# The 18 stores of attention's output tiles: issued from ScalarE's queue instead of SyncE's

## The chip, the core and the metric

The kernel runs on one core of one Trainium2 chip. The time is that of one whole execution in device microseconds. The kernel before took 623.82 us, the median of three runs (621.92, 623.82 and 624.80).

## What is computed

Two layers follow each other. The first is an attention with two branches over q, k and v of shape 4 x 8 x 576 x 64: a "down" branch, in which means over groups of four positions attend to each other and the result is repeated four times, and a "local" branch, in which each position attends to those less than four positions away. The two are added. The second is a mixture of experts over the 2304 resulting rows of 512 numbers: noisy logits choose two of eight experts for each row, and each expert is a two-layer network, 512 to 1024 to 512.

```python
out_up = np.repeat(sm_attn(q_d, k_d, v_d), 4, axis=2)
scores = np.where(abs(pos[:, None] - pos[None, :]) < 4, q @ k.T * scale, -1e9)
x = rows_of(out_up + softmax(scores) @ v)                 # 2304 x 512
noisy = x @ w_gate + log1p(exp(x @ w_noise)) * noise
for e in range(8):                                        # top 2 of 8 for each row
    out[mask] += weight * (relu(x[mask] @ w1[e]) @ w2[e])
```

## The kernel before

**Attention, about the first 166 us.** The local branch goes in 20 blocks of 116 positions, five for each of the four batches. A block is a chain over four engines: scores on TensorE (l_qk), maximum and difference on VectorE (l_max), exponent on ScalarE (l_exp), sum (l_sum), normalisation, transpose (l_pt), copy by ScalarE (l_ptc), product with v (l_pv, L689), and the sum with the down branch on VectorE (l_x, L711). The v rows of block n are the tile vw; they come in four loads of 64 KB each that l_load_v issues from SyncE's queue (L629). l_pv takes all four in its first few products.

Rows are put together to 18 output tiles of 128 rows. Each is transposed on TensorE (l_xt, L720), copied by ScalarE into a buffer x (l_xtc, L726), and stored into the DRAM tile x_d, 256 KB (l_store, L730). Three buffers x stand in a ring. Below, x3 is the store of tile 3, vw7 the v rows of block 7. The router's steps follow each group of tiles (r_soft, L758 and L759, with its two table loads, to r_put, which scatters list entries), and the experts' gathers read x_d.

**Experts.** Weights are fetched in 256 KB pieces (fetch_w, L219 and L222, tile raw), split on ScalarE (L229) and VectorE (L234), and used by TensorE to the end of the program. Six fills of 768 KB (fill_out, L194) zero the output in the attention stage.

**Order.** A planner (run_steps, L302) works out the order of all steps from costs and priorities when the program is built. Each engine then runs its own list strictly in that order: an instruction that waits holds up all behind it on its engine. keep_warm (L399) puts filler products on TensorE where the planner expects a gap.

**DMAs from SyncE and ScalarE.** Each of them adds to one of eight semaphores, DMAHW0 to DMAHW7, which are handed out in turn. An issue waits until the DMA before it on its own semaphore has landed, so that at most eight are under way. This wait is made where the program is built, beside the waits for data and buffers.

The step's record names SyncE, and its planned place doesn't change with the engine that issues it:

```python
s_store += [Step("l_store", "sp", 0.45, lambda n=ck: l_store(n), after=[a11], use=[xb], move=1.0, **kw)]   # L1026
```

Of the kernel before, what the change touches and what calls it, by code (L numbers as in the profile page):

```python
# [22 lines left out]
def kernel(  # L23
# [12 lines left out]
    nc = tc.nc  # L36
# [3 lines left out]
    P = 128  # L40
# [56 lines left out]
    x_rows = x_d.rearrange("(t a) c -> t (a c)", a=4)  # L97
# [348 lines left out]
    st = {}  # L446
# [280 lines left out]
        st["x", n] = x  # L727

    def l_store(n):
        nc.sync.dma_start(out=x_rows[n * P : (n + 1) * P, :], in_=st.pop(("x", n)).rearrange("p a c i -> p (a c i)"))  # L730

    def l_lg(n):
        xT = st["xT", n]
# [191 lines left out]
    for b in range(B):  # L925
# [71 lines left out]
        for i in range(NB):  # L997
            n = NB * b + i
# [20 lines left out]
            for ck, g, c, w in ps_:  # L1019
                if g + w < P:  # L1020
                    continue
                ptxb, xb, lgb, lsb, plb = (buf(x_) for x_ in ("tp", "x", RG, "lgT", RS))
                kw = dict(light=True, prio=n + KX)
                a10 = Step("l_xt", "pe", 0.46, lambda n=ck: l_xt(n), cols=512, after=[s_x], use=[xTb[ck]], new=[ptxb], **kw)
                a11 = Step("l_xtc", "act", 0.49, lambda n=ck: l_xtc(n), after=[a10], use=[ptxb], new=[xb], **kw)
                s_store += [Step("l_store", "sp", 0.45, lambda n=ck: l_store(n), after=[a11], use=[xb], move=1.0, **kw)]  # L1026
                a12 = Step("l_lg", "pe", 0.35, lambda n=ck: l_lg(n), cols=2048, after=[s_x, s_sel] + s_wgn, use=[xTb[ck]], new=[lgb, lsb], **kw)
                a12 = Step("l_lgt", "act", 0.18, lambda n=ck: l_lgt(n), after=[a12], use=[lgb, lsb], **kw)
                a12 = Step("l_ls", "pe", 0.25, lambda n=ck: l_ls(n), cols=64, after=[a12], use=[lsb], new=[plb], **kw)
                st["lg_args", ck] = (a12, plb, n)  # L1030
# [594 lines left out]
```

## Time and profile before

| | us |
|---|---|
| median of three runs | 623.82 |
| lowest and highest | 621.92, 624.80 |
| the profiled execution's own time | 620.2 |
| its span in the profile | 618.5 |

The profile shows one execution. Its span is 1.7 us shorter than that execution's own time, and its time is 3.6 us under the median. TensorE is busy for 589.4 us of the span, VectorE 403.8, ScalarE 333.7, GpSimd 237.7. Issuing a DMA isn't counted as busy; it has rows of its own, under SPq for SyncE. The granted clock of TensorE has two levels in the rows, 1.00 (2.4 GHz) and 0.50 (1.2 GHz); values between are a mean over a stretch with both.

### The profile page before, as it was taken

How to read it: one execution, taken by the hardware profiler on the slowest of the kernel's cores; microseconds unless marked ns; L12 is line 12 of the kernel's file. 1: busy time of each engine (PE TensorE's matmuls, PEld its weight loads, DVE VectorE, ACT ScalarE, POOL GpSimd, SP SyncE). 2: the span in 40 equal slices, each digit the busy share in tenths (PEclk: the TensorE clock that was granted, in tenths of full speed). 3: DMA queues.
4: the chain of work that ended last, by engine and by line, in shares of the span. 5: the costliest groups of instructions: out<-in, count | busy, mean ns of one | idle time of the engine just before them, and what ended most of it. 6: DMA issues, size and time to landing. Idle time of an engine off the chain costs nothing. (4 is left out here: it accounts for less than half of the span.)

```text
span 618.5 us, 12836 instructions
## 1 busy us (share of the span) xinstructions
PE 589.4 (95%) x4579; PEld 508.2 (82%) x4579; DVE 403.8 (65%) x1054; ACT 333.7 (54%) x786; POOL 237.7 (38%) x318
## 2 busy tenths in 40 slices
PE   8899998998997899999999999999999999999995
PEld 7677776766886789987998898799789789878985
DVE  5999797897765534676487367647846865784421
ACT  7977876775542412674386167337726645752400
POOL 7585567762536233232423233232333223132111
PEclk9999998898798899999999999999999999999998
DMA  9997897987556562544454364444445445344301
GB/s 191 187 182 147 209 196 152 238 178 208 164 121 77 145 196 83 158 142 153 134 157 128 119 193 142 153 132 143 132 141 172 136 152 175 113 146 130 110 24 48
DMA packets 136101, 91.39 MB, mean 148 GB/s; under 512 B 72107, under 2 KB 118699, under 8 KB 136028
## 3 DMA queue, kind: packets, MB, share of 16 engines
q1 hardware_dynamic: 126076, 62.72, 42.4%
q0 software_dynamic: 9952, 27.77, 14.2%
q8 instruction: 37, 0.61, 0.4%
q14 instruction: 36, 0.29, 0.2%
HBM read 71.38 MB, written 19.38 MB: 147 GB/s over the span
## 5 line engine op out<-in xcount | busy, mean ns | idle before, releaser
L1407 PE MATMUL py<-w1h,h 128*128 128x512 f32 (+4 forms) x544 | 168.9, 388 | 0.6 <-DVE ga L1415 0.6
L1366 PE MATMUL ph<-xh,w0h 128*128 128x288 f32 (+3 forms) x448 | 133.8, 299 | 0.9 <-ACT low L1412 0.7
L1366 PE MATMUL ph<-xh,w0l 128*128 128x288 f32 (+3 forms) x448 | 133.7, 298 | 0.0
L1366 PE MATMUL ph<-xl,w0h 128*128 128x288 f32 (+3 forms) x448 | 133.6, 298 | 0.0
L1407 PEld LDWEIGHTS py<-w1h,h 128*128 128x128 f32 (+3 forms) x544 | 99.4, 186 | 26.3 <-ACT w1h L229 1.2
L1407 PE MATMUL py<-w1l,h 128*128 128x512 f32 (+5 forms) x288 | 111.4, 389 | 0.0
L1375 ACT ACTIVATE h<-ph 128x512 fp32r<-128x512 f32 (+3 forms) x88 | 42.6, 484 | 113.5 <-PE ph L1366 80.7
L1416 POOL DMA_INDIRECT out_dram<-ga,lt x35 | 38.2, 1093 | 153.8 <-DVE ga L1415 116.7
L1376 DVE SCALAR_TENSOR_TENSOR h<-ph,h 128x512 fp32r<-128x512 f32 (+3 forms) x88 | 48.0, 546 | 63.4 <-ACT h L1375 63.2
L1366 PEld LDWEIGHTS ph<-xh,w0h 128*128 128x128 f32 x448 | 84.4, 188 | 2.1 <-ACT low L1412 1.1
L1366 PEld LDWEIGHTS ph<-xl,w0h 128*128 128x128 f32 x448 | 84.4, 188 | 0.3
L1366 PEld LDWEIGHTS ph<-xh,w0l 128*128 128x128 f32 x448 | 84.3, 188 | 0.0
L1282 ACT ACTIVATE xr<-tr 32x128 f32<-32x128 f32 x220 | 67.8, 308 | 3.1
L229 ACT ACTIVATE w0h<-raw 128x512 fp32r<-128x512 f32 x64 | 39.2, 625 | 53.0 <-DMA raw<-in_moe_w_dram 52.9
L1383 POOL DMA_INDIRECT ga<-out_dram,cl x35 | 35.9, 1026 | 73.3 <-PE ph L1366 56.4
L1407 PEld LDWEIGHTS py<-w1l,h 128*128 128x128 f32 (+4 forms) x288 | 51.8, 180 | 14.0 <-DVE w1l L234 1.3
L1154 POOL DMA_INDIRECT gx<-x_d,cl x35 | 36.7, 1048 | 53.0 <-PE ph L1366 27.0
L234 DVE TENSOR_TENSOR w1l<-raw,w1h 128x512 fp32r<-128x512 f32 x64 | 44.0, 688 | 18.7 <-ACT w1h L229 18.4
L1415 DVE SCALAR_TENSOR_TENSOR ga<-py,lt,ga 128x512 f32<-128x512 f32 (+4 forms) x32 | 23.4, 733 | 50.1 <-PE py L1407 50.1
L897 POOL DMA_INDIRECT list_d<-pay,sli x36 | 36.8, 1022 | 48.7 <-PE ptl L674 12.2
L1284 DVE COPY xr<-tr 32x128 f32<-32x128 f32 x220 | 50.4, 229 | 2.7
L229 ACT ACTIVATE w1h<-raw 128x512 fp32r<-128x512 f32 x64 | 40.1, 627 | 18.5 <-DMA raw<-in_moe_w_dram 17.9
(208 smaller groups left out, 1007.6 us busy)
## 6 DMA issues: line engine op xcount, KB each, us to landing
raw<-in_moe_w_dram SPq DMA_DIRECT2D x128, 256.0 KB
vw<-in_v_dram SPq DMA_DIRECT2D x80, 64.0 KB
x_d<-x SPq DMA_DIRECT2D x18, 256.0 KB
out_dram<-zero SPq DMA_DIRECT2D x6, 768.0 KB
nat<-in_q_dram SPq DMA_DIRECT2D x16, 256.0 KB
nat<-in_k_dram SPq DMA_DIRECT2D x16, 256.0 KB
vg<-in_v_dram SPq DMA_DIRECT2D x8, 320.0 KB
vg<-in_v_dram SPq DMA_DIRECT2D x8, 256.0 KB
```

Source lines behind the costliest of these rows:

```text
L229: nc.scalar.activation(hi, raw, AF.Copy)
L234: nc.vector.tensor_tensor(lo, raws.pop((e, z, f)), hi.bitcast(F32), op=ALU.subtract)
L897: ins = nc.gpsimd.indirect_dma_start(out=list_d[:, :], out_offset=bass.IndirectOffsetOnAxis(ap=sli[:, kk, i : i + 1], axis=0), in_=pay[:, ...
L1154: ins = nc.gpsimd.indirect_dma_start(out=gx[: got(e, t)], out_offset=None, in_=x_rows[:, :], in_offset=bass.IndirectOffsetOnAxis(ap=lists[ ...
L1282: nc.scalar.activation(dst, src, AF.Copy)
L1284: nc.vector.tensor_copy(dst, src)
L1366: last_mm[0] = nc.tensor.matmul(ph[:, n, 0:nh], lhsT=w[:, c, :], rhs=xx[:, c, sl], start=(c == 0 and z == 0), stop=(c == NDC - 1 and z == 2))
L1375: nc.scalar.activation(hh, src, AF.Relu)
L1376: nc.vector.scalar_tensor_tensor(out=hl, in0=src, scalar=0.0, in1=hh.bitcast(F32), op0=ALU.max, op1=ALU.subtract)
L1383: after_pe(nc.gpsimd.indirect_dma_start(out=acc[: tok(e, t)], out_offset=None, in_=out[:, :], in_offset=bass.IndirectOffsetOnAxis(ap=cl[: ...
L1407: last_mm[0] = nc.tensor.matmul(py[:rows, js], lhsT=hx, rhs=w[:, js], start=(f == 0 and z == 0), stop=(f == NFC - 1 and z == len(terms) - 1))
L1416: nc.gpsimd.indirect_dma_start(out=out[:, :], out_offset=bass.IndirectOffsetOnAxis(ap=lt[:m, t, 0:1], axis=0), in_=acc[:m], in_offset=None ...
```

## The change

One line: l_store issues from ScalarE's queue.

```diff
     def l_store(n):
-        nc.sync.dma_start(out=x_rows[n * P : (n + 1) * P, :], in_=st.pop(("x", n)).rearrange("p a c i -> p (a c i)"))
+        nc.scalar.dma_start(out=x_rows[n * P : (n + 1) * P, :], in_=st.pop(("x", n)).rearrange("p a c i -> p (a c i)"))
```

The lists of TensorE, VectorE and GpSimd are the same. ScalarE's gains 18 rows, SyncE's loses 18. The semaphores are handed out anew. In each row stand the semaphores that it waits for; a DMA's own is among them.

First place, blocks 6 to 8. SyncE before: x_1357 is the tile of store x3, vw_1372 is vw7, vw_1424 is vw8.

```order
L629 DMA vw_1293<-in_v_dram 64x4x64 [waits DMAHW2_49]
L455 DMA nat_0_0_1_1331<-in_q_dram 128x8x64 [waits DMAHW3_49,PE_49]
L505 DMA vg_0_1_1355<-in_v_dram 64x4x256 [waits DMAHW4_49,Pool_49]
L629 DMA vw_1372<-in_v_dram 64x4x64 [waits DMAHW5_49]
L629 DMA vw_1372<-in_v_dram 64x4x64 [waits DMAHW6_49]
L629 DMA vw_1372<-in_v_dram 64x4x64 [waits DMAHW7_49]
L629 DMA vw_1372<-in_v_dram 64x4x64 [waits DMAHW0_49]
L730 DMA x_d<-x_1357 128x512 [waits DMAHW1_49,Activation_49]
L629 DMA vw_1424<-in_v_dram 64x4x64 [waits DMAHW2_49,PE_49]
```

In the order of before the store x3 stands behind the four loads of vw7. SyncE now, from the last load before vw6 on:

```order
L455 DMA nat_0_0_0_1279<-in_q_dram 128x8x64 [waits DMAHW6_49,PE_49]
L629 DMA vw_1293<-in_v_dram 64x4x64 [waits DMAHW0_49]
L629 DMA vw_1293<-in_v_dram 64x4x64 [waits DMAHW1_49]
L629 DMA vw_1293<-in_v_dram 64x4x64 [waits DMAHW2_49]
L629 DMA vw_1293<-in_v_dram 64x4x64 [waits DMAHW3_49]
L455 DMA nat_0_0_1_1331<-in_q_dram 128x8x64 [waits DMAHW4_49,PE_49]
L505 DMA vg_0_1_1355<-in_v_dram 64x4x256 [waits DMAHW6_49,Pool_49]
L629 DMA vw_1372<-in_v_dram 64x4x64 [waits DMAHW7_49]
L629 DMA vw_1372<-in_v_dram 64x4x64 [waits DMAHW0_49]
L629 DMA vw_1372<-in_v_dram 64x4x64 [waits DMAHW1_49]
```

SyncE's turn skips 7 and 5: those are stores. ScalarE now, at the same place:

```order
L612 ACTIVATE up_1353<-od_1_1378 128x288 [waits PE_49]
L612 ACTIVATE up_1353<-od_2_1383 128x288 [waits PE_49]
L612 ACTIVATE up_1353<-od_3_1388 128x288 [waits PE_49]
L730 DMA x_d<-x_1357 128x512 [waits DMAHW7_49,Activation_49]
L792 ACTIVATE wts_1400<-wts_1400 128x8 [waits DVE_49]
```

The store x3 has semaphore 7, and the next DMA on 7 is the first load of vw7.

Second place, blocks 17 to 19. SyncE before: x_2777, x_2830 and x_2873 are the tiles of stores x12, x13 and x14, vw_2763 is vw18, vw_2847 is vw19.

```order
L629 DMA vw_2763<-in_v_dram 64x4x64 [waits DMAHW2_49,PE_49]
L629 DMA vw_2763<-in_v_dram 64x4x64 [waits DMAHW3_49]
L629 DMA vw_2763<-in_v_dram 64x4x64 [waits DMAHW4_49]
L629 DMA vw_2763<-in_v_dram 64x4x64 [waits DMAHW5_49]
L730 DMA x_d<-x_2777 128x512 [waits DMAHW6_49,Activation_49]
L629 DMA vw_2847<-in_v_dram 64x4x64 [waits DMAHW7_49,PE_49]
L629 DMA vw_2847<-in_v_dram 64x4x64 [waits DMAHW0_49]
L629 DMA vw_2847<-in_v_dram 64x4x64 [waits DMAHW1_49]
L629 DMA vw_2847<-in_v_dram 64x4x64 [waits DMAHW2_49]
L730 DMA x_d<-x_2830 128x512 [waits DMAHW3_49,Activation_49]
L730 DMA x_d<-x_2873 128x512 [waits DMAHW4_49,Activation_49]
```

Here x12 stands behind all of vw18, and x13 and x14 behind all of vw19. SyncE now, from the second of the last three fills on (vw_2673 is vw17):

```order
L194 DMA out_dram<-zero 1536x1x128 [waits DMAHW4_49]
L194 DMA out_dram<-zero 1536x1x128 [waits DMAHW6_49]
L629 DMA vw_2673<-in_v_dram 64x4x64 [waits DMAHW7_49,PE_49]
L629 DMA vw_2673<-in_v_dram 64x4x64 [waits DMAHW1_49]
L629 DMA vw_2673<-in_v_dram 64x4x64 [waits DMAHW3_49]
L629 DMA vw_2673<-in_v_dram 64x4x64 [waits DMAHW4_49]
L629 DMA vw_2763<-in_v_dram 64x4x64 [waits DMAHW5_49,PE_49]
L629 DMA vw_2763<-in_v_dram 64x4x64 [waits DMAHW6_49]
L629 DMA vw_2763<-in_v_dram 64x4x64 [waits DMAHW7_49]
L629 DMA vw_2763<-in_v_dram 64x4x64 [waits DMAHW0_49]
L629 DMA vw_2847<-in_v_dram 64x4x64 [waits DMAHW2_49,DMAHW1_49,PE_49]
L629 DMA vw_2847<-in_v_dram 64x4x64 [waits DMAHW2_49]
```

SyncE's turn now skips 5, 0 and 2. ScalarE now:

```order
L742 ACTIVATE lgT_2819<-pl_2814 128x128 [waits PE_49,Activation_49]
L730 DMA x_d<-x_2777 128x512 [waits DMAHW5_49,Activation_49]
L726 ACTIVATE x_2830<-ptx_2820 128x4x4x32 [waits DMAHW7_49,PE_49]
L726 ACTIVATE x_2873<-ptx_2860 128x4x4x32 [waits DMAHW3_49,PE_49]
L742 ACTIVATE lgT_2881<-pl_2876 128x128 [waits PE_49,Activation_49]
L758 ACTIVATE sp_2894<-lg_2852 128x16 [waits DVE_49]
L759 ACT_TABLE_LOAD
L759 ACTIVATE sp_2894<-sp_2894 128x16 [waits Activation_49]
L730 DMA x_d<-x_2830 128x512 [waits DMAHW0_49]
L730 DMA x_d<-x_2873 128x512 [waits DMAHW2_49]
L679 ACTIVATE pT_2887<-ptl_2882 128x512 [waits PE_49]
```

The stores x12, x13 and x14 have 5, 0 and 2. The next DMAs on these are the first and the fourth load of vw18 and the second of vw19, on SyncE.

## Rows read from the trace of the kernel before

**Rows 1.** The page: span, and busy time of each engine.

```profile
span 618.5 us, 12836 instructions
PE 589.4 (95%) x4579; PEld 508.2 (82%) x4579; DVE 403.8 (65%) x1054; ACT 333.7 (54%) x786; POOL 237.7 (38%) x318
```

**Rows 2.** Stretches: length, busy PE, PEld, DVE, ACT, POOL; clock, DMA share, GB/s.

```profile
55.00:166.00 111.00, 101.78 (x1432) 80.58 (x1429) 88.99 (x312) 78.16 (x186) 64.19 (x96) 0.91 0.82 192
166.00:210.00 44.00, 36.75 (x232) 33.07 (x230) 26.11 (x92) 17.22 (x35) 18.58 (x30) 0.95 0.56 103
210.00:618.50 408.50, 400.87 (x2317) 355.01 (x2316) 243.05 (x552) 195.02 (x460) 116.20 (x110) 0.99 0.44 136
```

**Rows 3.** Shorter stretches of attention, the same columns.

```profile
70.00:76.00 6.00, 6.00 (x74) 4.79 (x73) 4.78 (x22) 4.78 (x11) 2.54 (x4) 1.00 0.76 190
...
82.00:94.00 12.00, 11.81 (x161) 9.01 (x161) 11.18 (x35) 8.85 (x34) 8.05 (x12) 1.00 1.02 186
...
103.00:113.30 10.30, 7.47 (x47) 6.35 (x45) 6.34 (x24) 6.76 (x15) 5.38 (x9) 0.50 0.86 173
...
144.00:152.00 8.00, 7.44 (x154) 6.34 (x150) 7.03 (x35) 4.77 (x10) 2.11 (x3) 1.00 0.62 157
```

**Rows 4.** The store's line: count, ns least, median and most, first and last start.

```profile
L730 SPq DMA_DIRECT2D x_d<-x x18: 319/547/1327, 58.3 to 166.1; - x18
```

**Rows 5.** SyncE's issues in order of time: start and length in us, line, count.

```profile
70.89 3.23 SPq L629 DMA_DIRECT2D vw<-in_v_dram  x4
74.22 0.55 SPq L730 DMA_DIRECT2D x_d<-x  x1
...
83.71 0.80 SPq L730 DMA_DIRECT2D x_d<-x  x1
...
85.75 2.59 SPq L629 DMA_DIRECT2D vw<-in_v_dram  x4
...
90.62 2.15 SPq L629 DMA_DIRECT2D vw<-in_v_dram  x2
...
93.58 0.56 SPq L730 DMA_DIRECT2D x_d<-x  x1
...
98.23 1.33 SPq L730 DMA_DIRECT2D x_d<-x  x1
...
100.31 0.61 SPq L219 DMA_DIRECT2D raw<-in_moe_w_dram  x1
...
136.69 5.45 SPq L194 DMA_DIRECT2D out_dram<-zero  x3
...
145.98 1.28 SPq L629 DMA_DIRECT2D vw<-in_v_dram  x2
...
149.32 1.20 SPq L629 DMA_DIRECT2D vw<-in_v_dram  x1
```

**Rows 6.** SyncE's waits between 89 and 92 us: total, times, longest.

```profile
SPq L629 <- DMA x_d<-x: 0.8, 1, 0.8
```

**Rows 7.** ScalarE in order of time; in brackets idle time before, and its releaser.

```profile
71.69 0.99 ACT L612 ACTIVATE up<-od 128x288 f32<-128x288 f32 x3
...
105.63 0.63 ACT L229 ACTIVATE w0h<-raw 128x512 fp32r<-128x512 f32 x1 [4.89 <-DMA raw<-in_moe_w_dram]
...
135.05 0.23 ACT L759 ACTIVATE sp<-sp 128x32 f32<-128x32 f32 x1
...
151.02 0.22 ACT L759 ACTIVATE sp<-sp 128x16 f32<-128x16 f32 x1
```

**Rows 8.** TensorE in order of time, the products with v (l_pv).

```profile
78.16 1.14 PE L689 MATMUL o<-pT,vw 64*64 64x58 f32 x32
...
96.25 1.21 PE L689 MATMUL o<-pT,vw 64*64 64x58 f32 x28 [0.16 <-DMA vw<-in_v_dram]
...
149.44 1.14 PE L689 MATMUL o<-pT,vw 64*64 64x58 f32 x32
...
154.74 1.74 PE L689 MATMUL o<-pT,vw 64*64 64x58 f32 x26 [2.53 <-DMA vw<-in_v_dram]
```

## The prediction

> **What bounds the kernel now.** I read the busy line of the page first, then a table of stretches, then SyncE's, ScalarE's and TensorE's instructions in order of time around a few stores, and the waits of SyncE last. TensorE is busy for 95% of the span [rows 1]. Attention, 55 to 166 us, has TensorE busy for 101.8 of 111 us, and what follows for 36.8 of 44 and 400.9 of 408.5 [rows 2]. TensorE's list is fixed, and nearly all of it after 166 us hangs on attention, so what attention loses the whole kernel loses. ScalarE, which gets the stores, idles 33 of the 111 us (78.2 busy); VectorE idles 22. SyncE is the hidden one: it issues back to back for long stretches and each of its issues also waits for its semaphore. I therefore look less at what 18 issues cost than at which load now waits for which store.
>
> **What the change removes and adds.** SyncE loses 18 issues, median 0.547 us [rows 4]: 9.8 us. ScalarE gains 18 such issues. How long one takes there no row shows; I take SyncE's 0.55, bounds 0.32 and 1.33 [rows 4]. Each waits in its queue for two things: the copy l_xtc, which stands some instructions ahead on the same engine, and a load that was issued eight DMAs earlier and has landed when ScalarE gets there. So the stores hardly wait. They leave no later than before where SyncE was behind with them. Only loads, the list of SyncE, and behind them TensorE, can be late.
>
> The eight semaphores make them late. Before, a store took its place in SyncE's queue behind the loads of the same turn. Now the store takes an earlier place in the turn, and the load that comes eight later waits for it to land, while the store itself waits for ScalarE to arrive. At both places that the order shows, a load of v waits for a store which ScalarE reaches after SyncE would have issued that load.
>
> How long from the end of an issue to the landing? Least: vw17's last load ends its issue at 145.98 + 1.28 = 147.26 and is used at 149.44 without a wait, so 2.2 us at most [rows 5, 8]. vw18's last: 150.52 to 154.74, 4.2 us, waited for [rows 5, 8]. The raw weights: 100.92 to 105.63, 4.7 us [rows 5, 7]. Most: a store issued at 83.71 + 0.80 = 84.51, for which SyncE waited until 90.62, 6.1 us [rows 5, 6]. I use 2.2 to 6.1 as bounds. The short one belongs to a stretch with a DMA share of 0.62, the long one to a share of 1.02 [rows 3].
>
> *vw7.* The store x3 stands behind the three copies that end at 71.69 + 0.99 = 72.68 [rows 7]; issued by 73.2; the share there is 0.76 [rows 3], nearer to 0.62, so 2.5 us: landed at 75.7. vw7's first load started at 70.89 [rows 5]; now at 75.7, 4.8 us later. Four issues take 4 x 0.64 = 2.6 (two take 1.28 at 145.98, rows 5), to 78.3, and 2.2 more to land: 80.5. l_pv of block 7 started at 78.16 [rows 8], and TensorE is busy without a gap there (6.00 of 6.00, rows 3). **+2.3 us**; bounds 1.8 (issue of 0.32 and 2.2) and 9.8 (6.1 twice).
>
> *vw9.* SyncE goes on late. It catches up by three slots of stores that are gone, 0.55 for x3 [rows 5], the median 0.55 for x4 [rows 4], 0.80 for x5 [rows 5]: 1.9 of 4.8, so 2.9 late when vw9 is due (85.75, rows 5). vw9 had nothing to spare: TensorE waited for it at 96.25 [rows 8]. TensorE is itself 2.3 late by then. Net 0.6 at least; but the DMA engines are full there (1.02, rows 3), and a load that waits for another late load adds to it, up to 2.6. **+1.0**, bounds 0 and 2.6.
>
> *Raw weights: something is given back.* ScalarE idles 4.89 us at 105.63 for weights issued at 100.31 [rows 5, 7]. SyncE is rid of x6 and x7 before them, 0.56 + 1.33, so of its 2.9 about 1.0 is left there, while ScalarE is 3.3 late. The wait shrinks by the difference. **-2.0**, bounds 0 and -4.9.
>
> *vw17.* The first of three fills now waits for x11, which stands behind the table work that ends at 135.28 [rows 7]: with 1.3 of lateness so far, 0.55 and 2.5, 139.6 in place of 136.69 [rows 5]. That is 2.9 late, 1.6 more than TensorE, and vw17 stands behind the fills with nothing to spare at 149.44. The fills' issue is long (5.45 for three, rows 5), held up by full DMA engines, and takes up part. **+0.8**, bounds 0 and 2.9.
>
> *vw18, the largest.* Its last load waits for x13 to land. x13 stands behind the table work that ends at 151.02 + 0.22 = 151.24 [rows 7]; issued by 151.8, landed 2.2 later at 154.0, the load issued by 154.6, landed 4.2 later (what this very load took): 158.8. Before, TensorE got it at 154.74 after a wait of 2.53 [rows 8]. **+4.1**; bounds 2.1 (2.2 twice) and 9.9 (6.1 twice). Lateness from earlier places moves ScalarE and TensorE alike and doesn't enter.
>
> *ScalarE's own time.* 9.8 us of issues against 33 us of idle time; where it waits for TensorE or VectorE an issue costs nothing, and in the few dense runs the copies behind it come half a microsecond later. **+0.3**, bounds 0 and 9.8 (no issue hidden).
>
> The Trainium skill, "DMA: Bandwidth & Descriptors", section "Issuing engines are not separate DMA queues", says that issuing from a second engine only saves the sequencer's issue time, since all queues run on the same DMA engines. By that alone the change would be worth at most the slots above and never a loss; the order rows show what the rule leaves out, that a shared turn of semaphores ties the two queues together.
>
> **The sum.** 2.3 + 1.0 - 2.0 + 0.8 + 4.1 + 0.3 = 6.5 us. The profiled execution took 620.2, so 626.7 by its own measure; the median of the runs shown is 3.6 above it, 623.8, so I forecast **630.3 us**, with 625 to 636 as this case's own range (all low bounds but the give-back at its full size would even give -1.0; the high ends cannot all meet, since each late stretch empties the DMA engines for the next).
>
> **Rivals.**
> 1. *The lateness is taken up.* SyncE's late loads find emptier DMA engines and land in 2.2 us where they took 4.7 to 6.1. For it: a share of 1.02 just before vw9. Against it: vw18 sits in a stretch where even quick landings give +2.1. Only that and a little of vw7 is left beside the -2.0: +0.7, 624.5 us.
> 2. *Faster.* SyncE's freed slots bring the raw weights in early enough that ScalarE's idle 4.89 us goes and with it the stretch from 103.0 to 113.3 in which the granted clock is 0.50 (1.2 GHz) after TensorE had run out of work [rows 3, 7]. At full clock its 7.47 us of work are 3.7, and its 2.8 us of gap go: -6.5, 617.3 us. It decides if the raw load starts 4 us or more before 100.31 against ScalarE's list. For it: three stores, 2.7 us of issue (0.80, 0.56 and 1.33, rows 5), stood ahead of it from 83.71 on. Against it: the 4.8 us lost at vw7. The Trainium skill, "Perfetto Trace Analysis", section "DMA Optimizations", speaks for this one: it advises one issuing engine for inputs and another for outputs. No row of before bears it out for loads that share a turn with stores.
> 3. *Slower by the clock.* The new gaps at 78, 96 and 156 us are as long as those after which the clock fell in rows 3. Each such stretch costs 3.7 us (7.47 halved). Two of them on top of the forecast are 7.4 more, 637.7 us. Against it: a single gap may be under 2.5 us.
>
> **How the numbers follow.** Forecast 0.50, first rival 0.20, faster 0.13, clock 0.17. A measurement of this kernel tells about 0.5%, 3.1 us, from no change: faster is under 620.7, slower over 626.9. Faster: 0.13 of the second rival and 0.01 of the first, 0.14. Same: 0.16 of the first and 0.04 of the forecast, 0.20. Slower: the rest, 0.66. The range leaves out half of the faster case and some of the clock's: 619 to 638.
>
> **What would show it.** vw7's first load starts near 75.7 instead of 70.89, and rows of SyncE waiting for x_d<-x are there by the dozen. TensorE waits for vw at blocks 7, 9 and 18, the last for 6 us instead of 2.53. ScalarE's wait for raw falls from 4.89 to about 3. The first experts' products come 6 to 7 us later than at 166 us, and from there on the two traces run alike. If vw18's wait stays at 2.5 us, the largest term is wrong; if the low clock after 103 us is gone, the second rival has it.

## The result: 1.2% slower, as forecast

Eight runs of the changed kernel had a median of 630.28 us (626.51 to 631.88), eight of the kernel before 622.65 us (617.81 to 625.60). The ratio is 1.0124, with a 95% interval of 1.0082 to 1.0166, so +7.7 us (5.1 to 10.3). A second comparison later, of four runs with seven, gave 1.0161 (1.0102 to 1.0220). The profiled execution after took 631.72 us, the one before 620.2. They differ by 11.5 us, more than the medians do; a single profile is one draw from a range of several us, and the section on why comes back to this.

Page of the kernel after, its span and busy times. It answers to [rows 1].

```profile
span 629.8 us, 12832 instructions
PE 592.1 (94%) x4579; PEld 510.3 (81%) x4579; DVE 402.4 (64%) x1054; ACT 333.2 (53%) x786; POOL 236.9 (38%) x318
```

Stretches of the kernel after, with the limits of [rows 2] moved to where the same work stands now. Columns: length, busy PE, PEld, DVE, ACT, POOL; clock, DMA share, GB/s.

```profile
55.00:177.50 122.50, 105.75 (x1435) 82.96 (x1435) 87.28 (x312) 77.59 (x185) 63.80 (x96) 0.87 0.75 174
177.50:221.50 44.00, 36.07 (x233) 32.75 (x232) 25.21 (x92) 16.78 (x33) 18.13 (x30) 0.96 0.54 97
221.50:629.80 408.30, 400.28 (x2321) 354.34 (x2319) 244.22 (x554) 196.43 (x464) 115.94 (x110) 1.00 0.44 137
```

In this profile attention takes 122.5 us where it took 111, and what follows takes what it took: all is lost before 177.5 us. The DMA share fell from 0.82 to 0.75: the same 21.3 MB (192 GB/s x 111 us, 174 x 122.5) are moved over a longer time.

The store's line after, from its own view: count, ns least, median and most, first and last start. It answers to [rows 4].

```profile
L730 ACTq DMA_DIRECT2D x_d<-x x18: 326/326/589, 55.1 to 178.8; - x18
```

SyncE's issues after, in order of time (start, length, line, count), for [rows 5].

```profile
75.68 5.27 SPq L629 DMA_DIRECT2D vw<-in_v_dram  x8
...
89.30 15.12 SPq L629 DMA_DIRECT2D vw<-in_v_dram  x12
...
105.16 0.60 SPq L219 DMA_DIRECT2D raw<-in_moe_w_dram  x1
...
144.30 4.95 SPq L194 DMA_DIRECT2D out_dram<-zero  x3
149.35 17.34 SPq L629 DMA_DIRECT2D vw<-in_v_dram  x12
```

SyncE's waits of the kernel after between 50 and 180 us: total, times, longest.

```profile
SPq L629 <- DMA x_d<-x: 15.1, 7, 3.9
...
SPq L455 <- DMA x_d<-x: 3.9, 2, 3.6
```

The same view of the kernel before:

```profile
SPq L629 <- DMA x_d<-x: 1.2, 2, 0.8
```

SyncE now waits 19.0 us for stores, where it waited 1.2; in a second profile of the kernel before (e8 below) it is 0.7. vw7's first load starts at 75.68 instead of 70.89. The twelve loads of vw9 to vw11 take 15.12 us of SyncE; with a store between them they took 12.4 us in the first profile of before and 14.3 in e8, so little of that is new.

ScalarE of the kernel after, in order of time; the ACTq rows are the stores x3 and then x13 and x14.

```profile
71.66 0.39 ACT L612 ACTIVATE up<-od 128x288 f32<-128x288 f32 x1
71.71 0.33 ACTq L730 DMA_DIRECT2D x_d<-x  x1
71.95 0.70 ACT L612 ACTIVATE up<-od 128x288 f32<-128x288 f32 x2
...
112.44 0.63 ACT L229 ACTIVATE w0h<-raw 128x512 fp32r<-128x512 f32 x1 [5.50 <-DMA raw<-in_moe_w_dram]
...
158.38 1.28 ACT L759 ACT_TABLE_LOAD   x1
158.41 0.95 ACTq L730 DMA_DIRECT2D x_d<-x  x2
```

x3 is issued at 71.71 and SyncE's load starts at 75.68, when it has landed: 3.6 us from the end of the issue. ScalarE's wait for raw weights is 5.50 us where it was 4.89 [rows 7].

TensorE of the kernel after, the products with v that waited, for [rows 8].

```profile
80.23 1.02 PE L689 MATMUL o<-pT,vw 64*64 64x58 f32 x26 [0.43 <-DMA vw<-in_v_dram]
...
99.46 2.10 PE L689 MATMUL o<-pT,vw 64*64 64x58 f32 x30 [1.81 <-DMA vw<-in_v_dram]
...
165.06 0.47 PE L689 MATMUL o<-pT,vw 64*64 64x58 f32 x2 [4.26 <-DMA vw<-in_v_dram]
166.02 0.46 PE L689 MATMUL o<-pT,vw 64*64 64x58 f32 x2 [0.49 <-DMA vw<-in_v_dram]
167.66 1.75 PE L689 MATMUL o<-pT,vw 64*64 64x58 f32 x26 [1.18 <-DMA vw<-in_v_dram]
```

Block 18 now waits 4.26 + 0.49 + 1.18 = 5.9 us for v, in place of 2.53.

### The profile page after: what moved, and what is told of

Its sections match the earlier page's. It is cut to its first block, busy times and chain, and to the rows that moved or that the text cites. A ratio compares the mean times of both kernels' runs of the same rounds, so it can differ in the third digit from the quotient of the medians.

```text
span 629.8 us, 12832 instructions
## 1 busy us (share of the span) xinstructions
PE 592.1 (94%) x4579; PEld 510.3 (81%) x4579; DVE 402.4 (64%) x1054; ACT 333.2 (53%) x786; POOL 236.9 (38%) x318
## 3 DMA queue, kind: packets, MB, share of 16 engines
q0 software_dynamic: 9952, 27.77, 14.3%
```

## The experiments

The theory is that of the prediction: loads on SyncE wait for stores on ScalarE through the shared turn of eight semaphores. Rival A is ScalarE's time for 18 issues. Rival B is the stores' data, which leave on a queue of their own and meet the loads in the DMA engines. All ratios are to runs of the kernel before on the same chip.

### Six stores of each kind (e1, e2)

```diff
-        nc.sync.dma_start(out=x_rows[...], in_=...)
+        (nc.scalar if n in (1, 2, 9, 15, 16, 17) else nc.sync).dma_start(out=x_rows[...], in_=...)   # e1
+        (nc.scalar if n in (3, 4, 8, 12, 13, 14) else nc.sync).dma_start(out=x_rows[...], in_=...)   # e2
```

> Six stores (x1, x2, x9, x15, x16, x17) are issued from ScalarE, the other twelve from SyncE. By the trace of before each of the six is issued, with 2.2 us to land, before SyncE reaches the load that has the semaphore next (at most 0.1 us late). Theory (shared turn: loads wait for late stores): no loss, ratio to before 0.995 to 1.003, the products of block 7 and 18 start as in before (78.2 and 151.8, wait for v near 2.5 us at block 18). Rival A (ScalarE pays for issuing): a third of the loss of the full change, 2.5 us, ratio 1.004. Rival B (stores leave earlier and collide with loads): the same third.

> Six stores (x3, x4, x8, x12, x13, x14) are issued from ScalarE, the other twelve from SyncE. By the trace of before the loads that have the semaphores next are vw7 (4.5 us late), vw8 (3.2), vw13 (0.3), vw17 (3.2) and two of vw18 (5.3 and 4.6). Theory (shared turn): nearly the whole loss with a third of the stores: +2 us at block 7 and +5 to +8 at blocks 17 and 18, ratio 1.008 to 1.016. Rivals A (ScalarE's issue time) and B (earlier stores collide): like the six others, +2.5 us, ratio 1.004.

Measured: e1 1.0051 (1.0019 to 1.0084), e2 1.0070 (1.0045 to 1.0095). The pair doesn't tell the theories apart: e1 lost more than the theory said, e2 a little less, and the 1.004 of the rivals lies just under e2's interval. The six of e1 were not free. SyncE in e1, waits and issues between 60 and 75 us:

```profile
SPq L458 <- DMA x_d<-x: 4.6, 1, 4.6
```

```profile
63.34 0.60 SPq L458 DMA_DIRECT2D nat<-in_q_dram  x1
68.60 0.60 SPq L458 DMA_DIRECT2D nat<-in_k_dram  x1
```

The load after 63.34 shares with x2 and waited 4.6 us: x2 took 6.0 us from the end of its issue to landing, where 2.2 had been reckoned.

### ScalarE's time alone (e3)

```diff
         nc.sync.dma_start(out=x_rows[...], in_=...)
+        for _ in range(2):
+            nc.scalar.activation(junk, ident[:, 0:2], AF.Copy)
```

> All 18 stores stay on SyncE; at each store's place ScalarE gets two small ACTIVATEs on two columns instead, about 0.2 us each, 0.4 us a store against the 0.33 that an issue on ScalarE took. Rival A (ScalarE's time is what the change costs): +7 us, ratio 1.010 to 1.014. Theory (shared turn): 0 to +2 us, ratio 1.000 to 1.003.

Measured: 1.0016 (0.9982 to 1.0051), against 1.0124 for the change. The row shows that ScalarE had more to do than with the stores, 36 x 0.203 = 7.3 us against 18 x 0.326 = 5.9:

```profile
L733 ACT ACTIVATE junk<-ident x36: 187/203/226, 54.8 to 171.1; 128x2 f32<-128x2 f32 x36
```

Rival A falls as the main cause; at most 0.5% is left to it.

### The stores from GpSimd (e4), and the turn without the stores (e9)

GpSimd's DMAs have eight other semaphores of their own in these traces. e4 takes the stores out of the turn; e9 puts 18 DMAs of two numbers each, issued from ScalarE at the stores' places, back in. In e9's trace 226 of the first 228 DMAs of SyncE have the semaphore that they have in the change.

```diff
-        nc.sync.dma_start(out=x_rows[...], in_=...)
+        nc.scalar.dma_start(out=tie_d[n : n + 1, :], in_=st["x", n][0:1, 0, 0, 0:2])   # e9 alone
+        nc.gpsimd.dma_start(out=x_rows[...], in_=...)                                  # e4 and e9
```

> All 18 stores are issued from GpSimd, which has semaphores of its own for DMAs; SyncE's loads then share their turn with no store. Theory: no load of SyncE waits for a store; block 7 starts as in before or earlier, block 18 waits at most 2.5 us for v; what GpSimd pays for 18 issues (about 1 us each by its indirect ones) may come back elsewhere, ratio 0.99 to 1.01. Rival B (stores that leave earlier collide with loads in the DMA engines): the waits for v as in the changed kernel, 9 us over eight places, ratio 1.01 or more.

> The 18 stores go from GpSimd as in e4_pool (0.996 of before), but at each store's place ScalarE issues a DMA of two numbers from the same tile x into a scratch row. These take the places in the turn of the eight semaphores that the stores have in the changed kernel, load by load, and move no data to speak of. Theory (shared turn): the loss comes back without the stores, ratio to before 1.006 to 1.016; SyncE waits 8 to 19 us for the small DMAs, TensorE again for v. Rival B (a store on ScalarE's queue costs by its data, which shares the DMA engines with the loads): as e4_pool, ratio 0.993 to 1.000.

Measured: e4 0.9961 (0.9932 to 0.9989), e9 1.0074 (1.0042 to 1.0107). In e4 no load of SyncE waits for a store, TensorE has no wait for v among those listed after 50 us, and ScalarE's wait for raw weights is nearly gone. ScalarE's waits in e4 between 50 and 180 us, of that kind:

```profile
ACT w0h L229 <- DMA raw<-in_moe_w_dram: 1.2, 2, 1.1
```

In e9 SyncE waits again, 8.5 us for 36 numbers in all. SyncE's waits in e9, 50 to 180 us:

```profile
SPq L630 <- DMA tie_d<-x: 7.3, 5, 3.7
...
SPq L456 <- DMA tie_d<-x: 1.2, 1, 1.2
```

SyncE's issues in e9, with a hole of 3.7 us in front of vw7 where the change has one of 4.0, and then ScalarE's issue that SyncE waited for:

```profile
69.86 0.60 SPq L506 DMA_DIRECT2D vg<-in_v_dram  x1
74.16 5.30 SPq L630 DMA_DIRECT2D vw<-in_v_dram  x8
```

```profile
71.97 0.20 ACTq L731 DMA_DIRECT2D tie_d<-x  x1
```

Of the hole, 1.5 us went by until ScalarE issued the small DMA and 2.2 until it had landed. The stores' data and their place are those of e4, so 1.0074 / 0.9961 = 1.011 (about 1.007 to 1.016 by the two intervals), some 7 us, come with the small DMAs. They carry no data to speak of (rival B), and e3 says that ScalarE's time for them isn't it (rival A). What is left is the turn. This rests on the medians: the profiles are of the slowest of e4's twelve runs (625.24, median 619.18) and of the fastest of e9's (622.74, median 627.09), so they show who waits for whom, not what it costs. From e9 to the change there is another 1.0124 / 1.0074 = 1.005, which the two intervals don't set apart from 1: a whole store lands later than two numbers, and its data may cost something too; no run parts these.

### A few instructions later (e5)

```diff
     def l_ptc(n):
         nc.scalar.activation(st["pT", n], st.pop(("ptl", n)), AF.Copy)
+        put_stores()          # nc.scalar.dma_start of the tiles copied since
```

> All 18 stores are issued from ScalarE as in the changed kernel, but x0 to x14 a few instructions later in its list: behind the next copy l_ptc, and the last three at once. In the new turn no load is given the semaphore of a store that ScalarE reaches late, except the last load of vw7 (1.9 us late by the times of before, against 4.5 for its first) and one of vw19 (0.5). Theory (shared turn): most of the loss goes, ratio to before 0.994 to 1.004; SyncE waits for stores under 5 us in all, and block 18's wait for v is at most 3 us. Rival A (ScalarE's 18 issues): as slow as the changed kernel, ratio 1.010 to 1.015. Rival B (stores and loads collide): 1.006 to 1.015.

Measured: 1.0135 (1.0081 to 1.0189). The expectation failed: nothing was gained. SyncE waited 14.6 us for stores, not under 5. The largest of its waits, from a window of 104 to 112 us, and ScalarE at that time:

```profile
SPq L455 <- DMA x_d<-x: 6.5, 1, 6.5
```

```profile
104.08 0.60 ACT L477 ACTIVATE qT<-pt 128x512 f32<-128x512 f32 x1 [4.83 <-PE pt L466]
104.09 0.83 ACTq L740 DMA_DIRECT2D x_d<-x  x2
```

x6 and x7 stood behind a copy that waited 4.83 us for TensorE. A store put off in ScalarE's list takes over the waits of that list, and SyncE takes over the store's. The run doesn't separate the theories, since its premise, a turn without late stores, didn't come about.

### The early twelve and the late six (e6, e7)

As in e1, with n < 12 in e6 and n >= 12 in e7.

> Only x0 to x11 are issued from ScalarE; their turn up to the fills is that of the changed kernel, and no load of vw17 to vw19 shares with a store of ScalarE. Theory: the lateness before block 17 as in the changed kernel (+2 at block 7, +5 to +7 at block 11, +7 to +9 at block 16), without the +4 at block 18; ratio 1.006 to 1.011. Rival A: two thirds of the loss, 1.008, but spread evenly, 0.4 us a store.

> Only x12 to x17 are issued from ScalarE. Now x12 shares with the last load of vw17 (3.2 us late), x13 and x14 with the last two of vw18 (5.3 and 4.6). Theory: nothing moves before block 17, then +3 at block 17 and +2 to +4 at block 18: ratio 1.006 to 1.010 from six stores. Rival A: a third, 1.004.

Measured: e6 1.0138 (1.0089 to 1.0187), e7 1.0045 (1.0009 to 1.0082). Both are slower. By the medians most of the loss belongs to the first twelve, more than the theory had said, and the last six cost less than it had said; but both intervals overlap the theory's ranges, and they are too wide to add the two up.

### Both kernels once more (e8, e12)

> The kernel before once more, for a second profile of it: which of its waits repeat. Both theories: the start of block 7 within 0.5 us, the wait for vw18's last load between 1 and 4 us, ScalarE's wait for raw weights between 3 and 6 us; the time within 0.6% of 622.

> The changed kernel once more, for a second profile of it. What the shared turn causes must repeat: SyncE waits 10 to 20 us in all for stores, the products of block 7 end 1.3 to 2.3 us later than in both profiles of before, SyncE holds vw18's last load until x13 has landed, and from the end of block 16 to the end of block 18 at least 1 us more is lost than in the second profile of before (2.6 us). What is chance need not: the waits for v at blocks 9 and 10. Ratio to before 1.008 to 1.017.

Measured: e8 took 625.46 us; its wait at block 18 was 0.83 + 0.57 = 1.4 us, in reach of the 1 to 4 expected, and ScalarE's for raw weights 5.3. e12 has the ratio 1.0161 given above. Its block 7 lost 0.9 us and missed the 1.3 to 2.3; from the end of block 16 to that of block 18 it lost 5.2. SyncE's waits in e12 and then in e8, 50 to 180 us:

```profile
SPq L629 <- DMA x_d<-x: 15.6, 7, 5.2
...
SPq L455 <- DMA x_d<-x: 1.2, 1, 1.2
...
SPq L194 <- DMA x_d<-x: 0.4, 1, 0.4
```

```profile
SPq L629 <- DMA x_d<-x: 0.7, 1, 0.7
```

TensorE's waits for v in e12 and then in e8, same stretch:

```profile
PE o L689 <- DMA vw<-in_v_dram: 10.9, 8, 4.0
```

```profile
PE o L689 <- DMA vw<-in_v_dram: 3.9, 3, 2.5
```

So the change makes it 9.0 and 10.9 us where the two profiles of before have 2.7 and 3.9. These waits alone don't prove a loss, though: e3, in which no store is moved and whose profiled execution took 621.25 us, has

```profile
PE o L690 <- DMA vw<-in_v_dram: 7.0, 6, 2.6
```

What goes along with the loss is SyncE's wait for stores (50 to 180 us, in us; in e9 for the small DMAs). With one profile a run this is an order, not a law:

| run | SyncE's wait | TensorE's wait for v | ratio to before |
|---|---|---|---|
| before, e8 | 1.2, 0.7 | 2.7, 3.9 | 1 |
| e3, e4 (all stores on SyncE; all on GpSimd) | 0.6, none | 7.0, none | 1.0016, 0.9961 |
| e7 | 2.1 | 6.4 | 1.0045 |
| e1 | 6.8 | 6.2 | 1.0051 |
| e9 | 8.5 | 4.4 | 1.0074 |
| e6 | 8.8 | 9.1 | 1.0138 |
| e2 | 10.5 | 8.3 | 1.0070 |
| e5 | 14.6 | 5.9 | 1.0135 |
| the change, e12 | 19.0, 17.2 | 9.0, 10.9 | 1.0124, 1.0161 |

### Two attempts at a better kernel (e10, e11)

Both start from e4, the stores on GpSimd.

```diff
-        nc.sync.dma_start(out=rows, in_=zero...)                 # e10, fill_out
+        nc.gpsimd.dma_start(out=rows, in_=zero...)
-        Step("fill_out", ..., after=[s_fills], ...)              # e11
+        Step("fill_out", ..., after=[s_fills] + ([s_x] if f >= 3 else []), ...)
```

> The 18 stores and the six fills of 768 KB are issued from GpSimd, so SyncE holds loads alone. If the loads of v are late because SyncE is held up behind fills and stores: faster than with the stores alone, ratio to before 0.988 to 0.996. If the fills then crowd the DMA engines in front of the loads in the same way, or GpSimd pays for their descriptors: 0.995 to 1.005.

> The 18 stores are issued from GpSimd, and the last three fills are planned behind the last block of the local branch, so that vw17 to vw19 go ahead of them; the planner works the other steps out anew. If the fills are what makes vw17 and vw18 late: ratio 0.985 to 0.995. If the new order or the raw weights behind the fills cost as much: 0.995 to 1.01.

Measured: e10 0.9965 (0.9936 to 0.9995), e11 1.0015 (0.9986 to 1.0043). The fills gain nothing on top of e4, either way; in e11 the planner also built another order, so it says nothing of the fills alone. e4, all stores on GpSimd, is the fastest version of the study, by 0.4%, a little under what a run of few repeats can tell.

## Why the prediction was right, and where its terms were not

The forecast was +6.5 us, the ratio says +7.7 and, in the second comparison, about +10. Sign and mechanism were right, the places only in part. That the time forecast, 630.3 us, and the median measured, 630.28, agree so closely is luck: the kernel before came out at 622.65 in these runs, not at 623.82, and the change cost over 1 us more. The terms are checked on two profiles of each kernel (620.2 and 625.46 us before, 631.72 and 633.69 after), by how much later than in the first profile each block's last product with v ends. A row is the growth of that lateness over a stretch; the last column is the mean of the two after less the mean of the two before.

| stretch | e8 | after | e12 | predicted | measured |
|---|---|---|---|---|---|
| up to the end of block 6 | 0.2 | -0.1 | -0.1 | 0 | -0.2 |
| block 7 (vw7) | 0.0 | 2.0 | 0.9 | 2.3 | 1.5 |
| blocks 8 to 10 (vw9) | 4.9 | 4.0 | 6.8 | 1.0 | 2.9 |
| blocks 11 to 13 (raw weights) | 0.6 | 0.7 | 1.2 | -2.0 | 0.7 |
| blocks 14 to 16 | -2.0 | 2.2 | -2.8 | 0 | 0.7 |
| blocks 17 and 18 (vw17, vw18) | 2.6 | 4.0 | 5.2 | 4.9 | 3.3 |
| from there to the experts | -0.4 | -0.9 | 2.4 | 0.3 | 0.9 |
| sum | 5.9 | 12.0 | 13.5 | 6.5 | 9.8 |

With two profiles a side a row is good to two or three microseconds, since e8 alone, the same kernel, stands 5.9 us behind the first.

Two experiments lend a third profile of each side up to block 16: until then SyncE's loads have the semaphores of before in e7 and those of the change in e6. Their rows are 0.0 and 0.9 for block 7, 3.3 and 6.7 for blocks 8 to 10, -0.6 and -0.9 for blocks 11 to 13, -2.3 and 0.1 for blocks 14 to 16. So block 7 alone is clear of chance: 0.0 in each profile without the change, 0.9 to 2.0 with it. In blocks 8 to 10 the first profile of before, on which the forecast was built, was a good draw; the two others lose 4.9 and 3.3 us there without any change.

- *vw7* came as forecast: its first load started at 75.68, where 75.7 was forecast. That was luck, for two errors met there. The store was taken to leave at 73.2, behind three copies; it left at 71.71, while those copies were still to run, and then took 3.6 us to land, not 2.5. The row is 1.5, where 2.3 was forecast.
- *vw17 and vw18* were 4.9 together and came to 3.3; the place held in the first profile only. There x13 left by 158.74; SyncE's next load on its semaphore is vw18's last. Two narrow windows of SyncE in the kernel after:

```profile
157.93 2.14 SPq L629 DMA_DIRECT2D vw<-in_v_dram  x3
```

```profile
161.96 4.73 SPq L629 DMA_DIRECT2D vw<-in_v_dram  x5
```

  The second begins with that last load, 3.2 us after x13's issue ended, and TensorE's wait is 5.9 us, where 6 was forecast. In e12 the last load waited for x13 too, but TensorE's long wait stands at block 17, 4.03 + 1.34 us, and at block 18 it is 0.60:

```profile
159.45 0.63 PE L689 MATMUL o<-pT,vw 64*64 64x58 f32 x4 [4.03 <-DMA vw<-in_v_dram]
161.42 2.07 PE L689 MATMUL o<-pT,vw 64*64 64x58 f32 x28 [1.34 <-DMA vw<-in_v_dram]
...
165.59 2.00 PE L689 MATMUL o<-pT,vw 64*64 64x58 f32 x28 [0.60 <-DMA vw<-in_v_dram]
```

- *The raw weights* are the step that failed. I had SyncE 1.0 us late there, ScalarE 3.3, and 2.0 given back (the difference is 2.3; the sum has a slip of 0.3). The row is +0.7: nothing came back. Against the first profile SyncE was 4.85 late, 105.16 against 100.31 [rows 5], and ScalarE waited 5.50 us. But most of this isn't the change's doing. In e8, the kernel before, the same load leaves at

```profile
104.11 0.60 SPq L219 DMA_DIRECT2D raw<-in_moe_w_dram  x1
```

  In e12 it leaves at 105.95, and ScalarE waited 2.9 (e8: 5.3). On the means of two profiles, block 10 ends 4.2 us later than before and this load leaves 3.3 later, so SyncE gains under 1 us on the rest where 2.3 had been reckoned; ScalarE's wait falls from 5.1 to 4.2, and none of that reaches TensorE. Why it doesn't stays open.
- *vw9* was too small, 1.0 where the row is 2.9. What was mis-sized is the time to landing in the stretch with full DMA engines [rows 3]. x6 left by 90.06 + 0.33, and vw10's second load, which has its semaphore now, starts at 99.09:

```profile
99.09 3.94 SPq L629 DMA_DIRECT2D vw<-in_v_dram  x6
```

  That is 8.7 us, beyond the 6.1 that I had as the upper bound, and in e12 it is 10.7. Long landings there aren't new either. The rows of before had one that the prediction passed over: vw9's last load ended its issue at 85.75 + 2.59 = 88.34, and TensorE waited for vw9 until 96.25, which is 7.9 us [rows 5, 8]. In e8 the eight loads of vw9 and vw10 hold SyncE for 10.96 us, where the first profile has 7.7 from 85.75 on:

```profile
88.00 10.96 SPq L629 DMA_DIRECT2D vw<-in_v_dram  x8
```

  How much of the 2.9 is the change and how much the draw, these profiles don't settle. What vw9 and the raw weights lack in the forecast, 1.9 and 2.7 us, is made good in part by vw7, vw17 and vw18, which were 2.4 too large together.
- *ScalarE's own time* was rightly small: at most 0.5% by e3.
- *The first rival*, late loads that land sooner, isn't seen: in the first profile vw18's last load still left TensorE waiting 5.9 us.
- *The second*, a gain by the raw weights, has no more than a hint in e4: once the turn isn't shared, ScalarE's wait is 1.1 us at most and the kernel is 0.4% faster. That the one makes the other isn't shown: e10 waits 3.2 us for raw weights and has the same gain, e11 has no such wait among those listed and no gain. The Trainium skill, "Perfetto Trace Analysis", section "DMA Optimizations", says that it may make sense to give inputs one engine and outputs another. Here that gained about 0.4% with the outputs on GpSimd (e4) and cost 1.2% with them on ScalarE.
- *The third*, the clock, may have a share, but the prediction misread its row. It has the clock fall after TensorE had run out of work. In the kernel before, TensorE worked without a gap from 100 to 103 us at 1.00; the clock fell at 103.1, with the products of L604 still running, and the gap of 2.83 us came after that. A stretch, and TensorE in order of time:

```profile
100.00:103.00 3.00, 3.00 (x42) 1.62 (x39) 2.86 (x9) 0.74 (x2) 2.77 (x5) 1.00 0.82 186
```

```profile
100.28 3.50 PE L604 MATMUL od<-pts,vd 64*64 64x144 f32 x32
106.61 1.11 PE L720 MATMUL ptx<-ident,xT 128*128 128x128 f32 x4 [2.83 <-ACT up L612]
```

  In the kernel after the clock is 0.50 over other stretches. One of them, and then one of e8, where the kernel before has nearly the same:

```profile
99.30:106.00 6.70, 6.44 (x78) 5.47 (x78) 3.37 (x9) 1.63 (x4) 6.15 (x10) 0.50 0.35 71
```

```profile
98.40:105.20 6.80, 6.63 (x81) 5.70 (x82) 3.20 (x9) 1.33 (x3) 6.21 (x10) 0.50 0.47 134
```

  Between 50 and 200 us the clock is at 0.50 for 23.9 and 30.7 us in the two profiles of before and for 30.7 and 41.0 in the two of the change. That is 8.6 us more on the mean; if TensorE had work all through them, up to half of it, 4.3 of the 9.8 us, would be the clock's (an estimate). No run holds the waits without the clock, so its share is open.

## What to carry to other kernels

Before moving a DMA to another engine's queue, list which semaphore it will wait for and which later DMA will wait for it; where queues share a turn, a DMA that is issued late on one engine holds up loads on the other, however small it is. Price that with landing times from the same stretch, those of loads as well as of stores, not from a quieter one. And take a second profile of the kernel before, ahead of the forecast: blocks 8 to 10 differed by 4.9 us between two executions of the same program, more than any single term of this change, and a time that looks late against one profile may be an everyday one.

## What was not expected

- A DMA issue on ScalarE took 0.326 us (median of 18) where SyncE took 0.547 for the same store, and 0.20 for the two numbers of e9; SyncE's shortest was 0.319 [rows 4], so an issue needn't be longer there. It starts while work ahead of it in the list is still to run: x13 and x14 left at 158.41 beside a table load that ended at 159.66.
- Two numbers in a DMA held up SyncE for up to 3.7 us (e9), the wait until ScalarE issued it included; the longest wait for a 256 KB store was 3.9 us in the change and 5.2 in e12.
- From GpSimd the fills of 768 KB took about 1.1 us each to issue (e10), where SyncE was held 5.45 us for three [rows 5], yet nothing was gained by it.
